# A fused attention and MLP kernel: local attention's loads issued by GpSimd, buffers turning over in program order, new priorities

## The chip, the cores and the metric

The kernel runs on one core of one Trainium2 chip. The metric is device time in microseconds (us) of one execution, and the median of several executions is what is compared. A profiled execution has a time of its own, beside the span that its trace covers.

## What is computed

The inputs q, k and v have 4 batches, 8 heads, 576 tokens and head size 64. Attention is a sum of two parts: softmax attention over tokens averaged in fours (144 pooled tokens), repeated four times, and softmax attention within a band of |i - j| < 4. Its output, as 2304 tokens of 512, goes through two MLPs with weights 512 x 2048 and 2048 x 512. Everything is float32.

```python
q_d = q.reshape(B, H, Sd, factor, D).mean(axis=3)          # k_d, v_d alike
out_up = np.repeat(sm_attn(q_d, k_d, v_d), factor, axis=2)
mask = np.abs(pos[:, None] - pos[None, :]) < factor
scores = np.where(mask, scale * np.matmul(q, k.transpose(0, 1, 3, 2)), -1000000000.0)
out_local = softmax(scores) @ v
x = (out_up + out_local).transpose(0, 2, 1, 3).reshape(2304, 512)
h = x @ w_in;  x = (h * np.cos(h)) @ w_out
h = x @ w_in2; r = np.maximum(h, 0.0);  out = (r * r) @ w_out2
```

## The kernel before

**The work and its tiles.** Every float32 product of the MLPs is made of three matmuls, high by high, high by low and low by high part (`mm3`, L665 to 668), so weights and activations are first split in a high and a low part. The first MLP runs over five rounds of 256 to 512 tokens, and in each over 16 blocks `f` of 128 hidden columns: `mlp_h` gives h, ScalarE and VectorE make h cos(h), `mlp_o` adds the block's share of the output. The weights come as 64-bit words, and `convert` makes one block of them: a load of `rawi` (w_in) or `rawo` (w_out) by SP (L291), three VectorE steps (L295, L302, L307), a copy on ScalarE and a subtraction on VectorE (`split`, L273 and L276). The second MLP runs over three blocks of 768 tokens with seven products for a pair of blocks (`big_h`, `big_o`).

**Attention** is cut in units that stand between the blocks of the MLP rounds, since a round needs only the tokens that it works on. A pooled unit (`unit_g`, one batch and a pair of heads) is S (L504), softmax, transposes T (L520), pv (L538) and a repeat (L544). A local unit (`unit_l`, one batch and 116 of its tokens; five in a batch, here l0 to l4) is a mask matmul (L573), S (L579), softmax, T (L592), a copy into `pz` (L596), pv (L616) and the addition that gives x (L642). Batch 0 has all pooled units and its first local ones ahead of the first MLP matmul.

**Loads of attention.** `load_pooled` brings the four strided quarters that are summed for the pooled q, k and v. For batch 0, SP loads q and k (L358, eight loads) and VectorE adds them up (L368, L375, L379); v comes by four GpSimd loads (L398), of which each adds to what the one before left in `vd_sb`, so they follow each other. For batches 1 to 3 all twelve are such GpSimd loads, behind a small GpSimd copy (`gate`, L391) that waits for a step of the work. `load_local` (L403 to 419) brings a local unit's q (L407), its k in two halves `kz` (L411) and its v (L414). There are two buffers of each: `kz_70` and `kz_71` by the unit's parity, `q` and `v` in turn. So the load for a unit waits until the unit two earlier has used its buffer.

**What sets the order.** The program is not written in the order in which it runs. `Plan.op` registers each step with engine, cost, a priority `key`, what it reads and writes and which new buffers it takes; to the key a number from the table `OFF` is added, by the step's name and the stage of the program. `Plan.order` (L104 to 203) then plays all steps through a model of the engines: on each engine the step that can start goes, of several the one with the lowest key. Buffers of some kinds (`IN_TURN`) must be taken in a fixed turn, which is the order of the keys. Where the model finds TensorE idle ahead of the first `mlp_o`, it puts in matmuls of zeros with 128 columns (`busy`, L1173, the tile `idle`), here called fills. The steps are issued in the order that comes out:

```python
for _, i in plan.order():
    if i < 0:
        busy()
    else:
        plan.ops[i][3]()
```

Of the kernel before, what the change touches and what calls it, by code (L numbers as in the profile page):

```python
# [16 lines left out]
B, H, S, D = 4, 8, 576, 64  # L17
NT, DM, DFF = 2304, 512, 2048
PR = H // 2
# [3 lines left out]
QT = 58  # L23
# [29 lines left out]
STG = (36, 140, 300, 440)  # L53


class Plan:


    RATE = {"SP": 1.24, "POOL": 2.07}
    LAT = {"PE": 0.15, "ACT": 0.15, "DVE": 0.15, "SP": 0.0, "POOL": 0.0}  # L60

    IN_TURN = ("rawi", "rawo", "w2", "p", "pt", "q", "v", "t", "w1")

    def __init__(self, bufs):
        self.bufs = bufs
# [42 lines left out]
    def order(self):  # L108
        ops, n = self.ops, len(self.ops)
        after = [[] for _ in range(n)]  # L110
        left = [0] * n
        for i, o in enumerate(ops):
            left[i] = len(o[4])
            for j in o[4]:
                after[j].append(i)
        ready_at = [0.0] * n
        end = [None] * n
        begin = [None] * n
        free = dict.fromkeys(self.LAT, 0.0)
        got = {t: [] for t in self.bufs}  # L120
        cand = {e: [i for i in range(n) if ops[i][0] == e and not left[i]] for e in free}
        table = [None]
        dma = adding = 0.0
        used, warm = {}, {0: False}
        self.fill = []
        out = []
        turn = {t: [] for t in self.bufs}
        for i in sorted(range(n), key=lambda i: (ops[i][2], i)):
            for inst in ops[i][5]:
                turn[inst[0]].append(inst)  # L130

        stream = [x for o in sorted(ops, key=lambda o: o[2]) for x in o[5] if x[1] == "ws"]

        def room(inst, more=0):
            tag = inst[0]
            held = got[tag]
            at = len(held) + more
            if tag in self.IN_TURN and turn[tag][at] != inst:
                return None
            if inst[1] == "ws" and stream[0] != inst:  # L140
                return None
            if at < self.bufs[tag]:
                return 0.0
            last = [end[i] for i in self.users[held[at - self.bufs[tag]]]]
            return None if None in last else max(last) + 0.1

        while len(out) < n:
            best = None
            for e, c in cand.items():
                t_min, pick = None, []  # L150
                for i in c:
                    t = max(free[e], ready_at[i])
                    for j, inst in enumerate(ops[i][5]):
                        x = room(inst, sum(o[0] == inst[0] for o in ops[i][5][:j]))
                        t = None if x is None or t is None else max(t, x)
                    if t is not None:
                        pick.append((t, i))
                if not pick:
                    continue
                t_min = min(pick)[0]  # L160
                pick = [
                    (ops[i][2] + (4.0 if ops[i][6] not in (None, table[0]) else 0.0), t, i)
                    for t, i in pick if t <= t_min + 0.02
                ]
                k, t, i = min(pick)
                if best is None or (t, k) < best[:2]:
                    best = (t, k, i)
            assert best is not None, "the plan is stuck"
            t, _, i = best
            e, cost, _, _, _, new, tb = ops[i]  # L170
            for inst in new:
                got[inst[0]].append(inst)
                if inst[1] == "ws":
                    stream.pop(0)
            begin[i] = t
            if tb is not None and tb != table[0]:
                t += 1.3
                table[0] = tb
            if e in ("SP", "POOL"):
                cost *= self.RATE[e]  # L180
                if e == "SP":
                    free[e] = t + 0.5
                    dma = max(dma, free[e]) + cost
                    end[i] = dma + 1.6
                else:
                    free[e] = t + 1.0
                    adding = max(adding, free[e]) + cost * (1.3 if dma > t else 1.0)
                    dma = max(dma, t) + cost
                    end[i] = adding + 2.0
            else:  # L190
                if e == "PE":
                    x = max(free[e], 0.8)
                    while self.idle and t - x > 0.35:
                        self.fill.append(x)
                        x += self.slow(used, warm, x, FILL)
                    if ops[i][3] is self.last_fill:
                        self.idle = False
                    cost = self.slow(used, warm, t, cost)
                free[e] = end[i] = t + cost
            cand[e].remove(i)  # L200
            out.append(i)
            for j in after[i]:
                left[j] -= 1
                lat = 0.07 if ops[j][0] == e else self.LAT.get(e, 0.0)
                ready_at[j] = max(ready_at[j], end[i] + lat)
                if not left[j]:
                    cand[ops[j][0]].append(j)
        self.end = max(end)
        return sorted([(begin[i], i) for i in out] + [(x, -1) for x in self.fill])
# [15 lines left out]
def body(ctx: ExitStack, tc: tile.TileContext, qb, kw, vw, qp, kp, vp, wi, wo, masks, ident, out_t):  # L225
    nc = tc.nc
# [18 lines left out]
    kz = [att.tile([128, 2, 2, PR, KT], F32, name=f"kz{i}") for i in range(2)]  # L245
# [17 lines left out]
    op = plan.op  # L263
    T = {}

    def new(inst, shape, dtype=F32, space=None):
        p = psum if space else att if inst[0] in ATT else pool
        T[inst] = p.tile(shape, dtype, tag=inst[0], name=inst[0], bufs=BUFS[inst[0]])
        return T[inst]
# [133 lines left out]
    def load_local(b, d, key):  # L403
        q, v, kt = ("q", b, d), ("v", b, d), (b * ND + d) % 2

        def lq():
            nc.sync.dma_start(out=new(q, [128, 2, PR, QT]), in_=qb[b, d])  # L407

        def lk(hh):
            pp = slice(64 * hh, 64 * hh + 64)  # L410
            nc.sync.dma_start(out=kz[kt][pp, hh], in_=kw[b, d, pp])  # L411

        def lv():
            nc.sync.dma_start(out=new(v, [128, 2, PR, D]), in_=vw[b, d])  # L414

        op("SP", 0.68, key, lq, w=[q], new=[q])
        for hh in range(2):
            op("SP", 0.4, key, lambda hh=hh: lk(hh), w=[("kz", kt, hh)])
        op("SP", 0.75, key + 0.5, lv, w=[v], new=[v])
# [778 lines left out]
    for n, r in enumerate(ORDER):  # L1198
# [9 lines left out]
        for f in range(NF):  # L1208
# [3 lines left out]
            if not last and f == (GATE if first else 0):  # L1212
                e = need(r + 1)
# [12 lines left out]
    for R in range(NBIG):  # L1226
        if R:
            operands(R, big_when[R - 1, 1], big_when[R - 1, 2], big_step * 5)
        for p in range(PAIRS):
# [3 lines left out]
            q = (R, p - 1) if p else (R - 1, PAIRS - 1)  # L1233
# [83 lines left out]
```

## Time and profile before

| | |
|---|---|
| median of 3 runs | 943.61 us (941.19, 943.61, 946.57) |
| profiled execution, its own time | 936.85 us |
| its span | 935.0 us |
| TensorE (PE) busy | 912.2 us, 98% of the span |
| VectorE (DVE) busy | 624.6 us, 67% |
| ScalarE (ACT) busy | 421.2 us, 45% |
| GpSimd (POOL) busy | 36.7 us, 4% |
| granted TensorE clock | 0.998 of full speed |

Busy times are sums over instructions of one engine, from the profiled execution. A share is an average over stages: the first 66 us, up to the first matmul of the MLP, hold the fills, and a matmul of zeros counts as busy like any other. Starts of instructions are in us from the start of the span. DMA-issuing instructions of SP (SPq) are short and count as no work; those of GpSimd stand among its instructions.

### The profile page before, as it was taken

The numbers are of one execution on the slowest core, as the hardware profiler recorded it, in microseconds if no ns is written. First come the engines' busy times: TensorE is split into PE (matmuls) and PEld (weight loads), VectorE is DVE, ScalarE is ACT, GpSimd is POOL, SyncE is SP. The second block draws the span as 40 slices with busy tenths as digits, with TensorE's granted clock in tenths as the row PEclk, the third lists the DMA queues.
The fourth block names the chain that finished last, engine by engine and source line by source line (L and its number), as shares of the span: only waits on it lengthen the run. The fifth ranks groups of instructions, "written<-read, shape, count | busy, mean of one in ns | idle before, by whom it ended". The sixth has DMA issues, their size and how long they took to land.

```text
span 935.0 us, 15239 instructions
## 1 busy us (share of the span) xinstructions
PE 912.2 (98%) x5794; PEld 793.7 (85%) x5794; DVE 624.6 (67%) x1106; ACT 421.2 (45%) x865; POOL 36.7 (4%) x53
## 2 busy tenths in 40 slices
PE   9999999999999999999999989999999999999997
PEld 9787787789788877888888879999999898999996
DVE  6898789744754269867897667878955454635351
ACT  1866568767766376656665522213221111121111
POOL 3001200220030000000000000000000000000000
PEclk9999999999999999999999999999999999999999
DMA  9876956994892255776897796878776555766543
GB/s 286 272 215 191 251 181 224 287 249 154 257 194 80 71 171 163 258 257 219 290 324 234 247 337 219 291 242 266 243 257 199 183 180 178 212 226 183 168 158 113
DMA packets 82569, 204.10 MB, mean 218 GB/s; under 512 B 9281, under 2 KB 18241, under 8 KB 82497
## 3 DMA queue, kind: packets, MB, share of 16 engines
q1 hardware_dynamic: 77888, 191.33, 62.1%
q0 software_dynamic: 4608, 11.80, 6.6%
q8 instruction: 46, 0.75, 0.3%
q14 instruction: 27, 0.21, 0.1%
HBM read 162.20 MB, written 40.89 MB: 217 GB/s over the span
## 4 chain that ended last, share of the span: by engine, by line
PE 72%; DMA 2%; ACT 1%; DVE 1%; issue 0%; SPq 0%; ACTq 0%; DVEq 0%
PE acc L666 9%; PE acc L667 9%; PE acc L668 9%; PE pp L666 6%; PE pp L667 6%; PE pp L668 6%; PE ps L666 5%; PE ps L667 5%; PE ps L668 5%; PE acx L1094 2%; PE acx L1095 2%; PE acx L1093 2%; DMA w<-w_dram 1%; PE ps L579 1%; PE ps L616 1%; PE ps L520 0%
## 5 line engine op out<-in xcount | busy, mean ns | idle before, releaser
L666 PE MATMUL ps<-xh,w 128*128 128x512 f32 (+1 forms) x320 | 120.8, 377 | 2.5 <-DVE t L706 1.9
L666 PE MATMUL acc<-gh,w 128*128 128x512 f32 (+1 forms) x320 | 120.3, 376 | 0.7 <-DMA w<-w_dram 0.7
L668 PE MATMUL acc<-gh,w 128*128 128x512 f32 (+1 forms) x320 | 118.1, 369 | 1.0 <-DVE w L276 1.0
L667 PE MATMUL ps<-xl,w 128*128 128x512 f32 (+1 forms) x320 | 118.0, 369 | 0.5 <-DVE xl L276 0.5
L668 PE MATMUL ps<-xh,w 128*128 128x512 f32 (+1 forms) x320 | 117.8, 368 | 0.0
L667 PE MATMUL acc<-gl,w 128*128 128x512 f32 (+1 forms) x320 | 117.8, 368 | 0.0
L276 DVE TENSOR_TENSOR gl<-t,gh 128x512 fp32r<-128x512 f32 (+1 forms) x80 | 50.7, 635 | 46.4 <-ACT gh L273 45.6
L706 DVE TENSOR_TENSOR t<-t,ps 128x512 f32<-128x512 f32 (+1 forms) x80 | 50.5, 632 | 39.3 <-ACT t L703 39.1
L1066 DVE TENSOR_TENSOR xl<-c,xh 128x768 fp32r<-128x768 f32 x32 | 30.6, 956 | 68.4 <-ACT xh L1063 68.2
L666 PEld LDWEIGHTS ps<-xh,w 128*128 128x128 f32 x320 | 60.2, 188 | 16.4 <-DVE t L706 3.6
L668 PEld LDWEIGHTS acc<-gh,w 128*128 128x128 f32 x320 | 60.3, 188 | 12.0 <-DVE w L276 1.8
L666 PEld LDWEIGHTS acc<-gh,w 128*128 128x128 f32 x320 | 60.3, 188 | 11.9 <-issue 1.4
L1025 DVE TENSOR_TENSOR c<-ua,pp 128x384 f32<-128x384 f32 x96 | 52.8, 552 | 24.9 <-PE pp L668 21.4
L667 PEld LDWEIGHTS ps<-xl,w 128*128 128x128 f32 x320 | 60.3, 188 | 10.2 <-DVE xl L276 0.9
L1063 ACT ACTIVATE xh<-c 128x768 fp32r<-128x768 f32 x32 | 27.0, 845 | 93.0 <-PE acc L668 84.6
L668 PEld LDWEIGHTS ps<-xh,w 128*128 128x128 f32 x320 | 60.3, 188 | 10.1
L667 PEld LDWEIGHTS acc<-gl,w 128*128 128x128 f32 x320 | 60.4, 189 | 9.4
L711 ACT ACTIVATE t<-t 128x512 f32<-128x512 f32 (+1 forms) x80 | 46.7, 585 | 47.9 <-DVE t L698 46.9
L694 ACT ACTIVATE ki<-ps 128x512 int32<-128x512 f32 (+1 forms) x80 | 43.6, 550 | 43.5 <-PE ps L668 35.8
L273 ACT ACTIVATE gh<-t 128x512 fp32r<-128x512 f32 (+1 forms) x80 | 46.6, 583 | 32.1 <-PE acc L668 27.5
L698 DVE SCALAR_TENSOR_TENSOR t<-ki,ps 128x512 f32<-128x512 int32 (+1 forms) x80 | 50.0, 629 | 7.7 <-ACT ki L694 6.9
L703 ACT ACTIVATE t<-t,halfpi 128x512 f32<-128x512 f32 (+1 forms) x80 | 54.1, 678 | 1.8
(163 smaller groups left out, 2103.2 us busy)
## 6 DMA issues: line engine op xcount, KB each, us to landing
w<-w_dram SPq DMA_DIRECT2D x96, 512.0 KB, 3.7
gl<-w_dram SPq DMA_DIRECT2D x84, 256.0 KB, 3.2
gh<-w_dram SPq DMA_DIRECT2D x84, 256.0 KB, 3.7
rawi<-in_wi_dram SPq DMA_DIRECT2D x32, 512.0 KB, 6.0
rawo<-in_wo_dram SPq DMA_DIRECT2D x32, 512.0 KB, 5.7
w_dram<-w SPq DMA_DIRECT2D x32, 512.0 KB, 4.9
w_dram<-rawo SPq DMA_DIRECT2D x24, 512.0 KB, 4.2
v<-in_vw_dram SPq DMA_DIRECT2D x20, 256.0 KB, 4.2
```

The costliest lines, as they stand in the source:

```text
L273: nc.scalar.activation(out=hi(), in_=src(), func=AF.Copy)
L276: nc.vector.tensor_tensor(out=lo(), in0=src(), in1=hi().bitcast(F32), op=OP.subtract)
L666: nc.tensor.matmul(ps, w_hi, r_hi, start=first, stop=False)
L667: nc.tensor.matmul(ps, w_hi, r_lo, start=False, stop=False)
L668: nc.tensor.matmul(ps, w_lo, r_hi, start=False, stop=last)
L694: nc.scalar.activation(out=tt(ki), in_=tt(hp), func=AF.Copy, scale=1.0 / TWO_PI)
L698: nc.vector.scalar_tensor_tensor(out=tt(t), in0=tt(ki), scalar=-TWO_PI, in1=tt(hp), op0=OP.mult, op1=OP.add)
L703: nc.scalar.activation(out=tt(t), in_=tt(t), func=AF.Sin, scale=-1.0, bias=halfpi[:, 0:1])
L706: nc.vector.tensor_tensor(out=tt(t), in0=tt(t), in1=tt(hp), op=OP.mult)
L711: "ACT", act(n), key + 0.2, lambda: nc.scalar.activation(out=tt(t), in_=tt(t), func=AF.Abs), w=[t]
L1025: nc.vector.tensor_tensor(out=out(), in0=a(), in1=ps(), op=OP.subtract if sub else OP.add)
L1066: nc.vector.tensor_tensor(out=gpart(1, R, f), in0=T[t], in1=gpart(0, R, f).bitcast(F32), op=OP.subtract)
```

## The change

The loads of local attention go from SP's queue to GpSimd's. In the planner they are an engine `GQ` of their own that shares GpSimd's time. Buffers of the kinds in `IN_TURN`, and those of the second MLP (`stream`), turn over in the order in which the program registers the steps, not in the order of the keys. The table `OFF` has new numbers throughout (211 entries before, 206 after; one is shown). All lines behind the planner stand 5 further down.

```diff
-OFF = {('SP|body.<lambda>|wid', 0): -8.1,
+OFF = {('SP|body.<lambda>|wid', 0): -56.0,
...
-    RATE = {"SP": 1.24, "POOL": 2.07}
-    LAT = {"PE": 0.15, "ACT": 0.15, "DVE": 0.15, "SP": 0.0, "POOL": 0.0}
+    RATE = {"SP": 1.24, "POOL": 2.07, "GQ": 1.24}
+    LAT = {"PE": 0.15, "ACT": 0.15, "DVE": 0.15, "SP": 0.0, "POOL": 0.0, "GQ": 0.0}
...
-        for i in sorted(range(n), key=lambda i: (ops[i][2], i)):
-            for inst in ops[i][5]:
+        for o in ops:
+            for inst in o[5]:
                 turn[inst[0]].append(inst)
-        stream = [x for o in sorted(ops, key=lambda o: o[2]) for x in o[5] if x[1] == "ws"]
+        stream = [x for o in ops for x in o[5] if x[1] == "ws"]
...
-            if e in ("SP", "POOL"):
+            if e in self.RATE:
                 cost *= self.RATE[e]
...
+                elif e == "GQ":
+                    free[e] = free["POOL"] = t + 1.0
+                    beside = max(beside, free[e]) + cost * (2.0 if dma > t else 1.0)
+                    dma = max(dma, t) + cost
+                    end[i] = beside + 1.8
                 else:
-                    free[e] = t + 1.0
+                    free[e] = free["GQ"] = t + 1.0
...
-            nc.sync.dma_start(out=new(q, [128, 2, PR, QT]), in_=qb[b, d])
+            nc.gpsimd.dma_start(out=new(q, [128, 2, PR, QT]), in_=qb[b, d])
...
-            nc.sync.dma_start(out=kz[kt][pp, hh], in_=kw[b, d, pp])
+            nc.gpsimd.dma_start(out=kz[kt][pp, hh], in_=kw[b, d, pp])
...
-            nc.sync.dma_start(out=new(v, [128, 2, PR, D]), in_=vw[b, d])
+            nc.gpsimd.dma_start(out=new(v, [128, 2, PR, D]), in_=vw[b, d])
...
-        op("SP", 0.68, key, lq, w=[q], new=[q])
+        op("GQ", 0.68, key, lq, w=[q], new=[q])
         for hh in range(2):
-            op("SP", 0.4, key, lambda hh=hh: lk(hh), w=[("kz", kt, hh)])
-        op("SP", 0.75, key + 0.5, lv, w=[v], new=[v])
+            op("GQ", 0.4, key, lambda hh=hh: lk(hh), w=[("kz", kt, hh)])
+        op("GQ", 0.75, key + 0.5, lv, w=[v], new=[v])
```

What comes out of the planner is shown at three places. The first is the start of SP's queue, before. `v`, `q` and `kz` are loads of local units, `rawi` and `rawo` weights, `up_sb` and `xr` the pooled q and k of batch 0.

```order
L414 DMA v<-in_vw_dram 128x512 x2
L291 DMA rawi<-in_wi_dram 128x1024 x2
L291 DMA rawo<-in_wo_dram 128x1024 x2
L1178 DMA mask_f<-in_masks_dram 128x192
L1176 DMA id_sb<-in_ident_dram 128x128
L407 DMA q<-in_qb_dram 128x464 x2
L358 DMA up_sb<-in_qp_dram 128x4x144 x4
L358 DMA xr<-in_kp_dram 128x4x144 x4
L411 DMA kz_70<-in_kw_dram 64x512
```

And after:

```order
L363 DMA up_sb<-in_qp_dram 128x4x144 x4
L363 DMA xr<-in_kp_dram 128x4x144 x4
L296 DMA rawi<-in_wi_dram 128x1024 x2
L1181 DMA id_sb<-in_ident_dram 128x128
L1183 DMA mask_f<-in_masks_dram 128x192
L296 DMA rawo<-in_wo_dram 128x1024 x2
L296 DMA rawi<-in_wi_dram 128x1024 x2
L296 DMA rawo<-in_wo_dram 128x1024
L342 DMA w_dram<-w_177 128x1024
```

The eight loads of pooled q and k went from behind ten others to the front, and local attention's loads are gone from this queue.

The second is the start of GpSimd's queue, before: `vd_sb` is the pooled v of batch 0, the memsets clear the buffers of the local units.

```order
L398 DMA vd_sb<-in_vp_dram 72x1024
L1185 MEMSET kz_70 64x512 x2
L1185 MEMSET kz_71 64x512 x2
L1188 MEMSET pz_72 128x928
L398 DMA vd_sb<-in_vp_dram 72x1024
L1188 MEMSET pz_73 128x928
L398 DMA vd_sb<-in_vp_dram 72x1024 x2
```

And after:

```order
L1190 MEMSET kz_70 64x512 x2
L1190 MEMSET kz_71 64x512 x2
L403 DMA vd_sb<-in_vp_dram 72x1024
L419 DMA v<-in_vw_dram 128x512 x2
L416 DMA kz_70<-in_kw_dram 64x512 x2
L416 DMA kz_71<-in_kw_dram 64x512
L403 DMA vd_sb<-in_vp_dram 72x1024
L416 DMA kz_71<-in_kw_dram 64x512
L1193 MEMSET pz_72 128x928
L1193 MEMSET pz_73 128x928
L412 DMA q<-in_qb_dram 128x464 x2
L403 DMA vd_sb<-in_vp_dram 72x1024
```

The four memsets of `kz` now stand ahead of the first pooled v, and loads of the local units l0 and l1 stand between the four loads of the pooled v; the third `q`, which waits for S of l0, comes next and stands ahead of the fourth.

The third is TensorE's queue in batch 2, from S of l2 to S of l4, before:

```order
L579 MATMUL ps<-kz_70,q 58x128 x8
L592 MATMUL ps<-id_sb,p 128x128 x8
L573 LDWEIGHTS id_68
L573 MATMUL ps<-mask_69,id_68 128x512
L579 MATMUL ps<-kz_71,q 58x128 x8
L616 MATMUL ps<-pz_72,v 64x116 x8
L616 MATMUL ps<-pz_73,v 64x116 x8
L573 LDWEIGHTS id_68
L573 MATMUL ps<-mask_69,id_68 128x512
L579 MATMUL ps<-kz_70,q 58x128 x8
```

And after (`kz_70` is the buffer of l2 and l4, `kz_71` that of l3):

```order
L584 MATMUL ps<-kz_70,q 58x128 x8
L597 MATMUL ps<-id_sb,p 128x128 x4
L621 MATMUL ps<-pz_72,v 64x116 x8
L578 LDWEIGHTS id_68
L578 MATMUL ps<-mask_69,id_68 128x512
L584 MATMUL ps<-kz_71,q 58x128 x8
L621 MATMUL ps<-pz_73,v 64x116 x8
L597 MATMUL ps<-id_sb,p 128x128 x4
L578 LDWEIGHTS id_68
L578 MATMUL ps<-mask_69,id_68 128x512
L584 MATMUL ps<-kz_70,q 58x128 x8
```

Both pv used to stand behind S of l3; now one stands ahead of it, and four of the eight transposes behind it.

In all there are 654 fills before and 508 after. Of those, 646 and 498 come ahead of the first matmul of the MLP, 350 and 72 ahead of the first S, and 249 and 210 between the first pooled pv and the first matmul of the MLP. Ahead of the split of x for the first MLP round, VectorE's queue has 12 conversions of weight blocks before and 9 after.

## Rows read from the trace of the kernel before

**Rows 1.** Windows: us, busy time (instructions) of each engine, clock, DMA share, GB/s.

```profile
0.00:20.00 20.00, 19.01 (x293) 19.01 (x294) 12.55 (x28) 3.81 (x5) 6.33 (x13) 1.00 0.93 283
66.00:935.00 869.00, 850.53 (x4888) 737.54 (x4885) 571.52 (x989) 383.41 (x723) 29.51 (x39) 1.00 0.68 215
```

**Rows 2.** Timeline of TensorE, first 67 us: start, us, instruction, count [idle before, releaser].

```profile
0.99 22.36 PE L1174 MATMUL idle<-zero 128*128 128x128 bf16 x350 [0.99 <-DVE zero L1168]
24.13 1.88 PE L504 MATMUL ps<-kd_sb,qd_sb 128*96 128x144 f32 x12 [0.78 <-DVE kd_sb L368]
...
27.52 2.40 PE L1174 MATMUL idle<-zero 128*128 128x128 bf16 x40
...
33.37 0.71 PE L538 MATMUL ps<-pt,vd_sb 72*64 72x144 f32 x8
...
66.07 0.48 PE L666 MATMUL ps<-xh,w 128*128 128x512 f32 x1
```

**Rows 3.** Timeline of VectorE, 10 to 25 us.

```profile
12.30 0.42 DVE L295 TENSOR_SCALAR wm<-rawo 128x512 int32<-128x512 int32 x1
...
14.57 0.25 DVE L1192 CAST mask<-mask_f 128x192 bf16<-128x192 f32 x1
...
17.14 0.64 DVE L375 TENSOR_TENSOR up_sb<-up_sb 128x144 f32<-128x144 f32 x2
```

**Rows 4.** Timeline of GpSimd, first 24 us.

```profile
1.28 0.70 POOL L398 DMA_DIRECT2D vd_sb<-in_vp_dram  x1 [0.84 <-POOLq L1307]
2.03 2.22 POOL L1185 MEMSET kz<- 64x512 f32 x4
...
6.58 0.83 POOL L398 DMA_DIRECT2D vd_sb<-in_vp_dram  x1 [1.53 <-DMA vd_sb<-in_vp_dram]
...
15.11 0.83 POOL L398 DMA_DIRECT2D vd_sb<-in_vp_dram  x1 [6.81 <-DMA vd_sb<-in_vp_dram]
21.89 0.83 POOL L398 DMA_DIRECT2D vd_sb<-in_vp_dram  x1 [5.95 <-DMA vd_sb<-in_vp_dram]
```

**Rows 5.** Timeline of GpSimd around 85 and 251 us, pooled loads of batches 1 and 3.

```profile
85.24 0.59 POOL L398 DMA_DIRECT2D qn_sb<-in_qp_dram  x1
...
88.65 0.91 POOL L398 DMA_DIRECT2D qn_sb<-in_qp_dram  x1 [1.74 <-DMA qn_sb<-in_qp_dram]
...
251.24 0.57 POOL L398 DMA_DIRECT2D kd_sb<-in_kp_dram  x1 [0.37 <-issue]
...
256.87 0.89 POOL L398 DMA_DIRECT2D kd_sb<-in_kp_dram  x1 [3.97 <-DMA kd_sb<-in_kp_dram]
...
259.85 0.84 POOL L398 DMA_DIRECT2D vd_sb<-in_vp_dram  x1 [0.18 <-issue]
```

**Rows 6.** Window of 66 to 106 us.

```profile
66.00:106.00 40.00, 38.09 (x174) 30.56 (x172) 36.53 (x64) 24.85 (x41) 8.47 (x12) 1.00 0.74 208
```

**Rows 7.** Timeline of TensorE in batch 2, 238 to 249 us.

```profile
238.60 1.09 PE L579 MATMUL ps<-kz,q 128*58 128x128 f32 x16
239.62 0.69 PE L520 MATMUL ps<-id_sb,p 96*72 96x96 f32 x6
...
241.38 0.66 PE L538 MATMUL ps<-pt,vd_sb 72*64 72x144 f32 x8
241.97 0.44 PE L520 MATMUL ps<-id_sb,p 96*72 96x96 f32 x3
...
245.03 1.09 PE L579 MATMUL ps<-kz,q 128*58 128x128 f32 x16
246.04 1.09 PE L592 MATMUL ps<-id_sb,p 128*128 128x128 f32 x8
...
247.28 1.09 PE L579 MATMUL ps<-kz,q 128*58 128x128 f32 x16
248.20 1.00 PE L616 MATMUL ps<-pz,v 128*64 128x116 f32 x16
```

**Rows 8.** Timeline of SP's queue there.

```profile
239.73 0.33 SPq L407 DMA_DIRECT2D q<-in_qb_dram  x1
```

More of the change, by code (lines that the diff above doesn't have):

```diff
@@ L122, in order @@
         table = [None]
-        dma = adding = 0.0
+        dma = adding = beside = 0.0
         used, warm = {}, {0: False}
```

2 lines of the change are left out of this document (1 added, 1 removed).

## The prediction, made before the changed kernel was run

> **What bounds the kernel now.** The windows of the trace come first [rows 1]: between 66 us, where the first layer of the first MLP begins, and the end, TensorE is busy for 850.53 of 869.00 us at a granted clock of 1.00. So 18.5 us of idle time is all that anything behind the start could give back as idle, and the other 850 us are matmuls whose number the change leaves as it is. The start is different. The timeline of TensorE [rows 2] shows that its busy first 23 us are fills: 350 of the 128-column matmuls that only keep it busy. The first real one, S of pooled attention, begins at 24.13 and was released by VectorE's add of the pooled keys; the first pooled pv comes at 33.37 and the first matmul of the MLP at 66.07. What the change moves in the first 66 us, and what it does to the loads of local attention later, decides the time.
>
> The sum is made against the profiled execution, 936.85 us (span 935.0). The median of the three runs, 943.61, is 0.7% above it and the three lie between 941.19 and 946.57, so I work out a difference and carry it to the median. About 0.5%, 4.7 us, is what a measurement of this kernel can tell from no change.
>
> **1. The start.** Before, SP sends v, two w_in and two w_out blocks, mask, identity and q of two units, and only then the eight loads of pooled q and k; after, those eight are its first. Each is 128x4x144 numbers of 4 bytes, 0.29 MB, so q is 1.18 MB, which takes 4.2 us at the 283 GB/s of the first 20 us [rows 1]. VectorE's adds of q began at 17.14 and S was freed at 24.13 [rows 2, 3], 7.0 us later, other steps among them. From 1 us on this gives the first S at about 12 instead of 24.13. Its program agrees: 72 fills ahead of that S instead of 350.
>
> This is not yet a gain, for what is late next is the fourth load of the pooled v, without which no pooled pv runs. These four are a chain on GpSimd, each adding to the one before: issued at 1.28, 6.58, 15.11 and 21.89 [rows 4], 20.6 us from the first to the last. In the change the four memsets of 2.22 us come ahead of the first, which therefore goes out at about 3.5, and the fourth at 24.1. A mean step of the chain is 6.9 us, so it lands at about 31.0. The five issues of v and kz put between the first two cost 2.9 us at 0.57 (issues of loads that add nothing took 0.57 to 0.59 [rows 5]) and fit inside the first step of 5.3. From the first pooled pv to the MLP it took 32.7 us (33.37 to 66.07) [rows 2]; the program now has 39 fills fewer in that stretch, at 0.060 each (40 in 2.40 [rows 2]) 2.3 us, and one T of 0.5 us has moved ahead of it. 31.0 + 32.7 - 2.3 - 0.5 = 60.9 against 66.07: **-5.2 us**. Fills that stand in that wait cost nothing while they are shorter than it. Ends: all 148 fills that are left out ahead of the MLP were on the path, 148 x 0.060 = -8.9; or the 1.5 MB of local loads that GpSimd now sends between the first and third of the chain hold it up by their 5.4 us at 283 GB/s, +0.2.
>
> **2. Three weight conversions come later.** Ahead of the split of x for the first MLP, VectorE converts 12 weight blocks before and 9 after. One is four operations, from 12.30 to 14.57, 2.27 us [rows 3]; three are 6.8 us in the stretch of 66 to 106, where VectorE is busy for 36.53 of 40 us [rows 6], so 3.5 are free there. Ends: 0 (they wait until later, where VectorE has room: 571.52 of 869 us [rows 1]) and 6.8 - 3.5 = +3.3. Not all are due in that stretch; I take a third, **+1.0**.
>
> **3. Local attention's loads on GpSimd.** There are two q and two kz buffers, so the load for a unit waits for the S two units earlier. Before, for batch 2, S of unit 0 ends at 239.62, SP issues at 239.73, and S of unit 2 starts at 245.03 [rows 7, 8]: a turn of 5.4 us, just covered by what TensorE has between them. The change lets GpSimd issue the same three loads (q and two halves of kz). No row shows that; the nearest are its plain pooled loads, three in a row. At 251.24 the next link of the first went out after 5.6 us and that of the third after 8.6; at 85.24 the first took 3.4 [rows 5]. These three move 0.88 MB, a unit's three 0.50 MB, so I take 5.6, between ends of 3.4 and 8.6. Now the work between such pairs, in batch 2's order after, at the pitches of TensorE there [rows 7]: between unit 0 and 2 there are as many steps as before less one group of three plus seven transposes, 5.4 us; between 1 and 3 the eight pooled pv groups (2 x 0.59), T, mask and S (1.76), four and four transposes with a mask (1.24), a local pv (1.00), 5.2 us; between 2 and 4 the same 1.24, S 0.92, two local pv 2.0 and a mask 0.4, 4.6 us. A stall also lengthens the next interval: 0.2 for unit 2, 0.2 for unit 3, 5.6 - 4.6 - 0.2 = 0.8 for unit 4. Sum **+1.2**. In batches 1 and 3 the order leaves two or three more MLP groups in between, 6.3 us and more, and covers 5.6. Ends: at 3.4 nothing; at 8.6 3.2 + 0.2 + 3.8 in batch 2, 2.3 in batch 3 and about 1 in batch 1, +10.5.
>
> The Trainium skill bears on this in "SBUF — State Buffer", section "SBUF: two separate sides": GpSimd writes its own DMA descriptors and is kept from it while VectorE runs a two-port copy, so loads should go out on SP or ScalarE. Here GpSimd's plain issue took 0.59 us at 85.24 [rows 5] in a stretch with VectorE 91% busy [rows 6], which does not bear the rule out; it is priced as a rival.
>
> **4. The rest.** SP loses 80 issues, some 0.33 us each [rows 8], but TensorE has only those 18.5 us of idle time behind the start [rows 1], and no row shows any of it to hang on these issues; nothing is put down as gained. The turning over of buffers in program order changes neither the order of the second MLP's matmuls nor that of the tail: 0.
>
> Sum: -5.2 + 1.0 + 1.2 = -3.0. From the median this is 943.61 - 3.0 = **940.6 us**; the profiled execution would become 933.9.
>
> **Rivals.**
> **A. All of the start arrives.** The chain of pooled v runs faster because SP's 3.3 MB of other early loads no longer go ahead of it, conversions and turns hide: -8.9, 934.7 us. For it: the steps of 8.5 and 6.8 behind the first of 5.3 [rows 4] fall where SP's queue is full. Against it: the local loads now share GpSimd's queue. With some of the 18.5 us of idle time going too, down to 932.
> **B. The turns stall TensorE.** A GpSimd turn takes 8.6 us as its third load at 251 did [rows 5]: +10.5 and +1.0, less 5.2, is +6.3, 949.9 us. It is slower by over 4.7 from a turn of about 8.2 us on. Against it: 0.88 MB in those rows against 0.50. Without the gain at the start, 955.
> **C. The start stays at 66.** Queue order behind the pooled v, as bounded above: +0.2 + 1.0 + 1.2, 946 us.
> **D. VectorE slows the issues.** Adding loads show issues of 0.91 us against 0.59 [rows 5], 0.3 more; three in a turn make it 6.6: batch 2 loses 1.2 + 0.2 + 1.8, batch 3 0.3, together +3.5: 943.6 - 5.2 + 1.0 + 3.5 = 942.9 us. That is the rule of the Trainium skill's page; its own figures, about 620 ns alone and 3100 overlapped ("A bandwidth-pool intuition that's wrong"), would by an estimate from that page put 7.5 us on a turn and the time beyond B's.
>
> **How the numbers follow.** Forecast 0.36, A 0.34, B 0.16, C 0.09, D 0.05. The forecast's own spread (a few us both ways, between the ends of part 1) puts a small share of it, 0.03, below -4.7 and 0.02 above +4.7. Faster by over 0.5%: 0.34 + 0.03 = 0.37. Slower: 0.16 + 0.02 = 0.18. Within 0.5%: what is left of the forecast, 0.31, with C and D, 0.45. The range takes in A with its lower end and B: 932 to 951; left out are B without the gain at the start and what is faster than all fills, some 0.15.
>
> **What would show it.** In the changed profile: the first pooled S near 12, the first pooled pv near 31, its releaser the fourth pooled v; the first MLP matmul near 61. In the waits, TensorE waits for kz or q 1 to 2 us in all, in batch 2; plain GpSimd issues of about 0.6. VectorE's share in the 40 us behind the first MLP matmul goes up. Wrong would be: a first MLP matmul under 58 (A) or over 65 (C), waits for kz and q of over 8 us (B), or issues over 0.8 us (D), or a change behind 300 us, where I put nothing.

## The result and the profile after

The changed kernel takes 952.89 us (median of 6 runs, 948.96 to 956.31) against 943.74 us for the kernel before (6 runs, 939.12 to 946.57). The ratio is 1.0101, with a 95% interval of 1.0065 to 1.0136: it is slower by 1.0%, beyond the 940.6 us of the forecast and beyond its range. The profiled execution took 952.43 us (span 950.6), near its median, while that of the kernel before, 936.85, was a low one. So the two traces differ by 15.6 us where the medians differ by 9.2, and a stretch of one trace is compared below with several traces of the same order.

The first part of the page, after:

```profile
PE 911.5 (96%) x5648; PEld 791.2 (83%) x5648; DVE 623.7 (66%) x1106; ACT 423.9 (45%) x869; POOL 80.8 (8%) x133
```

TensorE's busy time hardly moved from 912.2 us, though 146 fills are gone: what is left runs longer, at a lower granted clock (0.988 of full speed in the mean, 0.998 before). Its idle time is 39.1 us against 22.8. The windows (columns as in [rows 1]) say where, for the start and for two stretches around 200 us:

```profile
0.00:70.00 70.00, 59.37 (x781) 53.47 (x782) 50.78 (x114) 37.19 (x142) 22.52 (x42) 0.95 0.82 236
180.00:200.00 20.00, 19.15 (x143) 18.83 (x144) 9.76 (x29) 11.19 (x27) 9.13 (x12) 0.91 0.83 171
200.00:210.00 10.00, 6.15 (x35) 5.98 (x35) 1.90 (x5) 2.88 (x8) 1.07 (x2) 0.70 1.00 255
```

In 0 to 70 us TensorE is idle for 10.6 us and its clock is 0.95; before, it was idle for 4.3 us at 1.00. From 200 to 210 us it is busy for 6.15 us only, at a clock of 0.70. TensorE's timeline in the first 66 us answers to [rows 2]:

```profile
0.99 6.54 PE L1179 MATMUL idle<-zero 128*128 128x128 bf16 x72 [0.99 <-DVE zero L1173]
15.17 3.19 PE L509 MATMUL ps<-kd_sb,qd_sb 128*96 128x144 f32 x12 [7.65 <-DVE kd_sb L373]
...
28.06 1.09 PE L584 MATMUL ps<-kz,q 128*58 128x128 f32 x16
29.08 5.92 PE L1179 MATMUL idle<-zero 128*128 128x128 bf16 x103
35.47 0.63 PE L597 MATMUL ps<-id_sb,p 128*128 128x128 f32 x4 [0.46 <-DVE p L478]
36.06 1.20 PE L543 MATMUL ps<-pt,vd_sb 72*64 72x144 f32 x16
...
65.83 0.47 PE L671 MATMUL ps<-xh,w 128*128 128x512 f32 x1
```

72 fills instead of 350, and then nothing for 7.65 us: the first S waits for the sums of the pooled k and starts at 15.17. Its twelve matmuls take 3.19 us where they took 1.88, since the clock had gone down in the wait (granted clock 0.50 from 13 to 19 us). The first pooled pv comes at 36.06, right behind T of l0 and without a wait of its own, later than the 33.37 of before, and the first matmul of the MLP at 65.83 against 66.07. GpSimd's timeline answers to [rows 4]:

```profile
2.90 0.69 POOL L403 DMA_DIRECT2D vd_sb<-in_vp_dram  x1
...
19.06 0.89 POOL L403 DMA_DIRECT2D vd_sb<-in_vp_dram  x1 [4.69 <-DMA vd_sb<-in_vp_dram]
29.45 0.56 POOL L412 DMA_DIRECT2D q<-in_qb_dram  x1 [9.50 <-PE ps L584]
30.00 0.90 POOL L403 DMA_DIRECT2D vd_sb<-in_vp_dram  x1
```

The third load of the pooled v goes out at 19.06, the fourth only at 30.00: the third `q` in front of it waited 9.50 us for S of l0. The list of TensorE's waits (us in total, times, longest):

```profile
PE ps L509 <- DVE kd_sb L373: 7.6, 1, 7.6
PE acc L671 <- DMA w<-w_dram: 3.8, 1, 3.8
PE acx L1098 <- DMA w<-w_dram: 3.7, 6, 1.1
PE ps L671 <- DVE t L711: 3.5, 4, 1.8
PE ps L671 <- ACT xh L278: 1.8, 1, 1.8
```

No wait for `q` or `kz` is in the list. The costly new one behind the start is a single wait of 3.8 us for a weight block.

To see where the time went, I read from each trace when the first matmul of the MLP starts, and when that of its third round (round 2, the first with 512 columns again behind the 256 of round 1) starts. The table has the results of all kernels tried below too; "old" and "new" tell whose order the steps stand in.

| kernel | order, local loads by | first MLP matmul | from it to round 2 | round 2 to the end | ratio to before |
|---|---|---|---|---|---|
| before | old, SP | 66.07 | 186.9 | 682.1 | 1 |
| e2_gq | old, GpSimd | 68.37 | 186.3 | 681.2 | 1.0005 |
| e6_turn | old, other turn, SP | 68.91 | 190.3 | 681.9 | 0.9992 |
| e12_before_no_adds | old, SP | 69.98 | 188.6 | 682.9 | 0.9995 |
| after | new, GpSimd | 65.83 | 199.7 | 685.1 | 1.0101 |
| e1_sp | new, SP | 65.22 | 199.2 | 686.9 | 1.0081 |
| e5_warm | new, GpSimd | 65.59 | 201.3 | 685.4 | 1.0098 |
| e10_late_local | new, GpSimd | 70.24 | 198.4 | 683.3 | 1.0117 |
| e11_no_adds | new, GpSimd | 64.75 | 192.7 | 684.2 | 1.0037 |
| e30_sp_early | new, SP | 66.24 | 192.8 | 684.4 | 1.0060 |
| e31_gq_early | new, GpSimd | 68.86 | 198.4 | 683.1 | 1.0101 |
| e20_stage2 | mixed, GpSimd | 67.78 | 197.6 | 685.1 | 1.0051 |
| e21_stage4 | mixed, GpSimd | 64.40 | 195.9 | 686.5 | 1.0102 |
| e22_start_only | mixed, GpSimd | 64.42 | 199.3 | 703.7 | 1.0290 |

The loss stands in rounds 0 and 1: from the first MLP matmul to round 2 it takes 198 to 201 us in after, e1_sp, e5_warm and e10_late_local, instead of 186 to 190 in the old order. Most of it is round 1, 86 us in after instead of 75. The end adds about 3 us. The start gives some 2 us back: in the seven traces that have the new start unchanged (all new and mixed ones but e5_warm, e10_late_local and e22_start_only) the first MLP matmul comes at 64.4 to 68.9, 66.2 in the mean, in the four of the old order at 66.1 to 70.0, 68.3 in the mean. Before's own is the earliest of these four.

### The profile page after: what moved, and what is told of

It is laid out like the page before. It is cut to its first block, busy times and chain, and to the rows that moved or that the text cites. A ratio compares the mean times of both kernels' runs of the same rounds, so it can differ in the third digit from the quotient of the medians.

```text
span 950.6 us, 15033 instructions
## 1 busy us (share of the span) xinstructions
PE 911.5 (96%) x5648; PEld 791.2 (83%) x5648; DVE 623.7 (66%) x1106; ACT 423.9 (45%) x869; POOL 80.8 (8%) x133
## 4 chain that ended last, share of the span: by engine, by line
PE 77%; DMA 8%; DVE 8%; ACT 6%; issue 1%; SPq 0%; DVEq 0%; ACTq 0%
PE acc L671 10%; PE acc L673 10%; PE acc L672 10%; PE ps L671 6%; PE ps L672 6%; PE ps L673 6%; PE pp L671 6%; PE pp L673 5%; PE pp L672 5%; DMA w<-w_dram 4%; PE acx L1098 2%; PE acx L1099 2%; PE acx L1100 2%; ACT p L456 1%; PE ps L621 1%; PE idle L1179 1%
## 5 line engine op out<-in xcount | busy, mean ns | idle before, releaser
L671 PE MATMUL acc<-gh,w 128*128 128x512 f32 (+1 forms) x320 | 122.3, 382 | 5.9 <-DMA w<-w_dram 3.8
L673 PE MATMUL acc<-gh,w 128*128 128x512 f32 (+1 forms) x320 | 119.5, 373 | 0.8 <-DVE w L281 0.8
L671 PEld LDWEIGHTS ps<-xh,w 128*128 128x128 f32 x320 | 61.6, 193 | 18.5 <-DVE t L711 5.5
L673 PEld LDWEIGHTS ps<-xh,w 128*128 128x128 f32 x320 | 61.6, 192 | 10.1
L1030 DVE TENSOR_TENSOR ua<-ua,pp 128x384 f32<-128x384 f32 x72 | 39.8, 552 | 32.8 <-PE pp L673 29.7
```

Source lines behind the costliest of these rows:

```text
L671: nc.tensor.matmul(ps, w_hi, r_hi, start=first, stop=False)
L673: nc.tensor.matmul(ps, w_lo, r_hi, start=False, stop=last)
L1030: nc.vector.tensor_tensor(out=out(), in0=a(), in1=ps(), op=OP.subtract if sub else OP.add)
```

## The experiments

**Queue or order.** Two kernels split the change: the new order with SP's loads, and the old order with GpSimd's.

```diff
-            nc.gpsimd.dma_start(out=new(q, [128, 2, PR, QT]), in_=qb[b, d])
+            nc.sync.dma_start(out=new(q, [128, 2, PR, QT]), in_=qb[b, d])
...
```

(`kz` and `v` alike; in the second kernel the other way round, in the kernel before.)

> The changed kernel with its own order, but local attention's loads issued by SP again, at the places that they have in the program's order. TensorE's, VectorE's and ScalarE's queues are those of the changed kernel. Theory order (the new order of the steps costs the time, above all in the second round of the first MLP): stays within 0.4% of the changed kernel, ratio to before 1.007 to 1.014, TensorE again waits 2 us or more for a weight block near 205 us, and the first MLP matmul of the third round comes near 265 us. Theory queue (GpSimd's slower issue or landing costs it): ratio to before at most 1.003 and the third round near 255 us.

> The kernel before with its own order, but local attention's loads issued by GpSimd. Theory order: within 0.3% of before (0.997 to 1.003), no wait of TensorE for q or kz above 1 us in all. Theory queue: 1.006 or more, with waits of TensorE for q, kz or v, or for the pooled v whose chain stands on the same queue.

Measured: 1.0081 (1.0049 to 1.0112) for the new order with SP's loads, 1.0005 (0.9987 to 1.0022) for the old order with GpSimd's. The queue costs nothing that can be told, in either order; the loss comes with the order. In the trace of the first, the wait for a weight block was 1.94 us, just under the 2 us expected, and round 2 starts at 264.4; in that of the second, TensorE waits for `kz` for 1.0 us in all, the bound that I had given. The tile `q` in the trace after and in that before tells why the queue is harmless: GpSimd's issue takes 0.57 us (median), and from issue to landing it is as fast as SP.

```profile
L412 POOL DMA_DIRECT2D q<-in_qb_dram x20: 536/565/928, 12.9 to 365.4; - x20
...
DMA to landing us min/median/max: 2.8/4.2/9.2
```

```profile
L407 SPq DMA_DIRECT2D q<-in_qb_dram x20: 327/338/756, 5.5 to 352.1; - x20
...
DMA to landing us min/median/max: 2.6/4.4/9.7
```

**The turning over alone**, in the kernel before:

```diff
-        for i in sorted(range(n), key=lambda i: (ops[i][2], i)):
-            for inst in ops[i][5]:
+        for o in ops:
+            for inst in o[5]:
...
-        stream = [x for o in sorted(ops, key=lambda o: o[2]) for x in o[5] if x[1] == "ws"]
+        stream = [x for o in ops for x in o[5] if x[1] == "ws"]
```

> The kernel before with buffers turning over in program order, its table of priorities and SP's loads as before. Theory order, the table alone: the rule of turning over matters little under the old table, ratio 0.997 to 1.004. Rival: the rule itself makes steps wait for their buffer's turn, ratio 1.005 or more, with longer waits of TensorE for weights.

Measured 0.9992 (0.9974 to 1.0011). So what makes the order is left: the new table of priorities, together with the planner's engine `GQ`. No kernel here takes these two apart.

**The adding loads beside the weights.** In the trace after, the weight block that TensorE waits for from 201.65 to 205.50 us is asked for at 196.49 and lands 8.88 us later. SP's queue, the DMA view of 185 to 210 us (queues: packets, MB, share of the 16 engines; then issues, KB each, median us to landing), and TensorE's timeline there:

```profile
196.49 13.54 SPq L350 DMA_DIRECT2D w<-w_dram  x4
```

```profile
q0 software_dynamic: 1307, 3.17, 72.9%
q1 hardware_dynamic: 430, 1.57, 18.1%
...
w<-w_dram SPq DMA_DIRECT2D x4, 512.0 KB, 9.4
kd_sb<-in_kp_dram POOLq DMA_DIRECT2D x3, 288.0 KB, 5.8
vd_sb<-in_vp_dram POOLq DMA_DIRECT2D x3, 288.0 KB, 6.7
qn_sb<-in_qp_dram POOLq DMA_DIRECT2D x3, 288.0 KB, 7.5
```

```profile
201.37 0.28 PE L673 MATMUL ps<-xh,w 128*128 128x256 f32 x1
205.50 0.55 PE L671 MATMUL acc<-gh,w 128*128 128x256 f32 x1 [3.85 <-DMA w<-w_dram]
205.84 0.41 PE L672 MATMUL acc<-gl,w 128*128 128x256 f32 x1
206.06 0.41 PE L673 MATMUL acc<-gh,w 128*128 128x256 f32 x1
...
210.75 0.28 PE L671 MATMUL ps<-xh,w 128*128 128x256 f32 x1
210.87 0.28 PE L672 MATMUL ps<-xl,w 128*128 128x256 f32 x1
```

Pooled q, k and v of batch 2, nine of whose twelve loads add to what is there, hold 72.9% of the DMA engines' time, and a weight block takes 9.4 us. Behind the wait of 3.85 us the 256-column matmuls come 0.21 us apart instead of 0.12 for 5 us, at the lower of the clock's two levels (1.2 instead of 2.4 GHz). I left the nine adding loads out, in the changed kernel and, as a control, in the kernel before:

```diff
-                    "POOL", 0.82, key, lambda dst=dst, src=src, r=r, how=how: nc.gpsimd.dma_start(
+                    "POOL", 0.82, key, lambda dst=dst, src=src, r=r, how=how: None if b == 2 and r else nc.gpsimd.dma_start(
```

> The changed kernel without the nine adding loads of batch 2's pooled q, k and v (their sums are left out, only the first quarter is loaded). Theory contention (these loads, which run from 186 to 206 us, slow the weight block that TensorE waits 3.8 us for at 205 us, and the clock is at half for about 5 us behind that wait): the wait falls under 1 us, the granted clock of 200 to 210 us rises from 0.70 to 1.00, and the time falls by 4 to 7 us, ratio to before 1.003 to 1.006. Rival (the block is asked for too late in the new order, whatever else is loaded): the wait stays above 2.5 us and the time within 2 us of the changed kernel.

> The kernel before without the same nine adding loads of batch 2's pooled q, k and v (their sums are left out). Theory contention through order (the old order has the same loads, but keeps the weight blocks clear of them): the time falls by less than 2.5 us, ratio to before 0.997 to 1.001, and round 1 to round 2 stays at 74 to 76 us. Rival (the adding loads cost 6 us wherever they stand, and the new order has nothing to do with it): 4 us or more are gained, ratio 0.996 or below, round 1 to round 2 in 71 us or less.

Measured: 1.0037 (1.0014 to 1.0060) in the new order, 944.61 us, and 0.9995 (0.9981 to 1.0010) in the old one. The same nine loads cost 6 us in the one (some 2 to 10, going by the two intervals) and under 2 in the other. The window and the weight loads of the changed kernel without them:

```profile
200.00:210.00 10.00, 9.37 (x75) 8.90 (x74) 4.24 (x11) 4.77 (x12) 0.00 (x0) 1.00 0.43 154
```

```profile
w<-w_dram SPq DMA_DIRECT2D x6, 512.0 KB, 3.3
```

The clock is back at 1.00, the wait is gone and a block lands in 3.3 us.

Why the loads cost nothing in the old order is not what I had expected there, that it keeps the weight blocks clear of them. In the trace before, three weight blocks are asked for from 194.67 on, while the adding loads still run. GpSimd's last of them and SP's queue, then how long these three blocks took to land and, below it, the same for the three from 196.49 on in the trace after:

```profile
198.06 0.84 POOL L398 DMA_DIRECT2D vd_sb<-in_vp_dram  x1 [1.03 <-DMA vd_sb<-in_vp_dram]
```

```profile
194.67 3.19 SPq L345 DMA_DIRECT2D w<-w_dram  x3
```

```profile
DMA to landing us min/median/max: 6.9/8.4/11.3
```

```profile
DMA to landing us min/median/max: 8.9/9.8/10.2
```

And TensorE's timeline before, where the first and the last of the three are first used:

```profile
204.09 0.28 PE L666 MATMUL acc<-gh,w 128*128 128x256 f32 x1
...
208.93 0.39 PE L666 MATMUL acc<-gh,w 128*128 128x256 f32 x1 [0.32 <-DMA w<-w_dram]
```

So the blocks land late in both orders. What differs is how long TensorE has other work: in the old order the first block is used 9.4 us after it was asked for, two local pv and four transposes being among what stands in between, and only the third is waited for, 0.32 us. In the new order the block is wanted 5.2 us after it was asked for (201.65 less 196.49), and takes 8.9. That this lead decides is read from the traces; no kernel here changes it alone.

**Moving them earlier.** If it is their place, 10 us earlier should help. In the new order their gate waits for a softmax of batch 1's third local unit and opens at 181.67 (174.17 before); the last pooled pv that reads their buffers is done at 172.

```diff
-        for _, i in plan.order():
+        line = [i for _, i in plan.order()]
+        adds = [i for i in line if i >= 0 and i in early]
+        last = max(line.index(i) for i in range(adds[0]) if ("pv", i) in reads)
+        for i in adds:
+            line.remove(i)
+        line[last + 1:last + 1] = adds
+        for i in line:
```

(`early` holds batch 2's pooled loads, `reads` batch 1's pooled pv; batch 2's gate copy is dropped.)

> The kernel of the first experiment (changed order, local attention's loads on SP), with batch 2's twelve pooled loads taken off their gate and put right behind the last pooled pv of batch 1, the last step that reads their buffers: they can run from 172 us instead of 182. Theory contention (what the new order costs is mostly these loads beside the weight loads of round 1): they end by 194 to 198 us, before or with the first weight loads at 196, TensorE's wait there goes from 2 to 4 us to under 1, round 1 to round 2 takes 78 to 81 us instead of 85, and the time falls by 3 to 6 us, ratio to before 1.002 to 1.005. Rival (they only move their contention onto loads ahead of them): ratio 1.007 or more, other waits for DMA in place of that one.

> The same with the changed kernel itself, its local loads on GpSimd: the loads of the last units of batch 1 now stand behind the adding loads on GpSimd's queue. Theory contention: as with SP's loads, ratio 1.002 to 1.006, since the q, kz and v behind them are wanted only 20 us later. Rival (one queue in order: TensorE waits for q, kz or v of these units): more than 1 us of such waits and a ratio above 1.008.

Measured: 1.0060 (1.0037 to 1.0083) with SP's local loads, against 1.0081 without the move, and 1.0101 (1.0077 to 1.0125) with GpSimd's. The first did in its trace what was expected (the block lands in 6.1 us, the wait is 1.06 us, from the MLP's start to round 2 it takes 6 us less), but its median fell by 2.4 us only, less than the 3 to 6 expected, and the intervals overlap; its trace, 945.17 us, is below its median of 947.48, and that of e1_sp, 953.12, above its own of 949.89. So that the place of these loads costs time is not shown by it, though the trace points that way. The second did not: TensorE waits as before, and not for the local loads but for the weights.

```profile
207.88 0.55 PE L676 MATMUL acc<-gh,w 128*128 128x256 f32 x1 [4.19 <-DMA w<-w_dram]
```

```profile
kz<-in_kw_dram POOLq DMA_DIRECT2D x4, 128.0 KB, 13.4
...
q<-in_qb_dram POOLq DMA_DIRECT2D x2, 232.0 KB, 12.6
```

On GpSimd's queue in order, seven local loads stood behind the adding ones, went out together from 197.05 on, and came into the DMA engines beside the same weight blocks: `kz` took 13.4 us to land. Here the queue did matter, in the trace; in the times the two intervals, 1.0037 to 1.0083 and 1.0077 to 1.0125, just overlap.

**The start.** Two kernels on the new order: the eight early local loads put behind the third load of the pooled v, and 110 more fills behind the first 72.

```diff
-        for _, i in plan.order():
+        line = [i for _, i in plan.order()]
+        own = [i for i in line if i >= 0 and plan.ops[i][0] in ("POOL", "GQ")]
+        adds = [i for i in own if plan.ops[i][0] == "POOL" and plan.ops[i][1] > 0][:4]
+        held = [i for i in own if plan.ops[i][0] == "GQ" and own.index(i) < own.index(adds[2])]
+        for i in held:
+            line.remove(i)
+        at = line.index(adds[2]) + 1
+        line[at:at] = held
```

```diff
+                seen += 1
+                if seen == 72:
+                    for _ in range(110):
+                        busy()
```

> The changed kernel, but the eight loads of local attention that GpSimd issues ahead of its third load of the pooled v go behind that one. Theory start (these loads take the DMA engines from the pooled k that SP asked for first): the first pooled S comes at 10 to 12 us instead of 15.2, and TensorE's 7.6 us wait there shrinks to 3 or 4; but the first MLP matmul moves by less than 2 us, because then S of the first local unit waits for q or kz, as it does with SP's loads. Rival (the pooled k is late for SP's own queue): the first S stays at 14 us or later. Rival two (the late pooled k alone holds the start): the first MLP matmul at 62 us or earlier. Time within 0.4% of the changed kernel unless rival two holds, then 3 to 4 us less.

> The changed kernel with 110 more fills behind the first 72, in the 7.6 us in which TensorE waits for the pooled k. Theory: the first S still starts at 14 to 16 us, since it waits for VectorE's sums, but at the full clock, so that its twelve matmuls take 1.9 us instead of 3.2 and the first MLP matmul comes 1 to 2 us earlier, at 63.5 to 65; granted clock of the first 70 us 0.98 or more instead of 0.95; ratio to before 1.006 to 1.011. Rival (these fills are on the path): the first MLP matmul 3 us or more later. Rival two (the fills the plan left out were worth nothing, warm or cold): the same time within 0.5 us at the first MLP matmul.

With the local loads held back the first S came at 10.08, as expected: they had taken the DMA engines from the pooled k. But S of l0 then waited 8.40 us for its `q`, more than expected, and the MLP started at 70.24 instead of within 2 us of 65.83; ratio 1.0117 (1.0087 to 1.0147).

```profile
10.08 0.98 PE L509 MATMUL ps<-kd_sb,qd_sb 128*96 128x144 f32 x6 [3.32 <-DVE kd_sb L373]
...
31.42 1.97 PE L584 MATMUL ps<-kz,q 128*58 128x128 f32 x16 [8.40 <-DMA q<-in_qb_dram]
...
40.43 1.20 PE L543 MATMUL ps<-pt,vd_sb 72*64 72x144 f32 x16
```

With SP's loads (e1_sp) it was the same in small: S at 10.58, a wait of 4.31 us for `q`, the MLP at 65.22. With more fills the clock stayed at 1.00 and six matmuls of S took 0.93 us (the first S came at 13.13, ahead of the 14 to 16 expected), but the MLP came at 65.59, 0.2 us earlier: rival two of that run. Its pv waited for the pooled v:

```profile
13.13 0.93 PE L509 MATMUL ps<-kd_sb,qd_sb 128*96 128x144 f32 x6
...
36.13 1.20 PE L543 MATMUL ps<-pt,vd_sb 72*64 72x144 f32 x16 [0.28 <-DMA vd_sb<-in_vp_dram]
```

So in the trace after three chains end within 1 us of each other: the fills behind S of l0 at 35.00, the softmax of l0 at 35.32, which T of l0 waits for, and the fourth pooled v, which lands at 35.93. Taking one away shows the next. In e1_sp, where no `q` stands ahead of it, the fourth pooled v goes out at 26.40 and lands 4.6 us later, at 31.0, and the pooled pv still starts at 35.39, behind the fills and T of l0:

```profile
26.40 0.82 POOL L403 DMA_DIRECT2D vd_sb<-in_vp_dram  x1 [7.73 <-DMA vd_sb<-in_vp_dram]
```

```profile
28.37 6.64 PE L1179 MATMUL idle<-zero 128*128 128x128 bf16 x103
34.85 0.61 PE L597 MATMUL ps<-id_sb,p 128*128 128x128 f32 x4
35.39 1.20 PE L543 MATMUL ps<-pt,vd_sb 72*64 72x144 f32 x16
```
The ratio with more fills is 1.0098 (1.0064 to 1.0133), the same as the changed kernel.

**Which numbers of the table.** Three kernels take the numbers of some stages from the old table: those of rounds 1 and 2, those of the second MLP, and all but those of the start. One entry of the first:

```diff
-('GQ|load_local.lq|q|wq', 2): 9.4,
+('GQ|load_local.lq|q|wq', 2): 126.7,
...
```

> The changed kernel, but the table's 39 numbers for the steps of rounds 1 and 2 of the first MLP (its second and third) are those of before; GpSimd's loads, the turning over and the rest of the table stay. If the second round's order is what costs (theory order, with the adding loads of batch 2 beside the weight loads as its largest part), the stretch from the first matmul of round 1 to that of round 2 falls from 86 us to 75 to 79, and the time by 6 to 11 us, ratio to before 0.998 to 1.004. Rival (the loss comes from rounds 0 and the start, and would turn up anywhere): the stretch stays above 83 us and the ratio above 1.007.

> The changed kernel, but the table's numbers for the second MLP are those of before. From the last first-layer matmul of the first MLP to the end it took 410 to 412 us in kernels with the new order and 407 with the old: if these numbers do it, 407 to 408 and ratio to before 1.004 to 1.008; if it is something earlier that shifts the loads there, 410 or more and 1.008 to 1.013.

> The changed kernel, but all of the table except the numbers for the start (what comes ahead of the first MLP matmul) is that of before; GpSimd's loads and the turning over stay. Theory order: 0.996 to 1.003, the first MLP matmul at 64 to 67 us, since the new start gains nothing there, and round 1 to round 2 in 75 to 79 us. Rival (the new start is worth its 5 us and only what follows gave it back): the first MLP matmul by 62 us and ratio 0.996 or below.

Old numbers for rounds 1 and 2 gave 1.0051 (1.0031 to 1.0070), half of the loss; the stretch from round 1 to round 2 took 81.7 us, above the 75 to 79 expected (its trace, 952.32 us, is the longest of its twelve executions). Old numbers for the second MLP gave 1.0102 (1.0059 to 1.0145): no gain, and 411 us for the last part, so my reading of the 3 us there fell. All old but the start gave 1.0290 (1.0256 to 1.0323), which neither theory had: the first MLP matmul at 64.42 as expected, but then new waits that neither kernel has.

```profile
130.66 0.80 PE L671 MATMUL ps<-xh,w 128*128 128x512 f32 x1 [5.06 <-DVE t L711]
```

```profile
469.68 1.09 PE L597 MATMUL ps<-id_sb,p 128*128 128x128 f32 x4 [4.72 <-DVE p L478]
```

In this last kernel the old numbers behind a new start make waits of their own, so mixing is no way to tell stages apart, and the half that e20_stage2 gives is not more than a hint.

## Why the prediction was wrong

**Part 4 failed: "the rest", 0 us.** I priced the three edits of the diff and what they moved at the start and in the local units, and put nothing on the new order in rounds 0 and 1 of the first MLP. My first paragraph asked only how much of the 18.5 us of idle time could be given back, and took the 850 us of matmuls behind the start as fixed; both can also grow. That is where 13 us of the traces' 15.6 went (9 to 13 against the traces of the old order). Without batch 2's adding loads the new order loses 0.4% instead of 1.0%, and the old order loses nothing by them. So about two thirds of the loss, by the middle values, comes of these loads in the new order. They meet round 1's weight blocks in both orders, and the blocks land 7 to 11 us after they are asked for; but in the new order TensorE wants the first of them after 5.2 us instead of 9.4. That a wait there also lowers the clock added to it: 3.85 us of idle, and then some 5 us of matmuls at almost half the pace (granted clock 0.50). The rows for it were in the trace of before: the three blocks from 194.67 on, which landed up to 11.3 us after they were asked for, covered by other work. I used the chains of adding loads [rows 4, 5] to price a turn of local loads, and did not ask what else would be loading when they ran, and how soon TensorE would want it.

**Part 1 failed too: -5.2, measured -0.2** in these two traces, and some -2 in the mean of the traces of either order. From the first pooled pv to the MLP I worked out 29.9 us and it took 29.8. Two steps failed. One is "the fourth at 24.1": I shifted the old spacing of the chain by the memsets, and left out that a `q` which waits for S of l0 stands right ahead of that load in the same queue, so that it went out at 30.00. The other is the path itself, that the pooled pv starts when this load lands. In e1_sp it lands at 31.0, the very time that I had worked out, and the pv starts at 35.39: T of l0 had moved ahead of that pv, as I had noted, and I priced its 0.5 us but not the softmax that it waits for, nor the fills. The first S at 12 came at 15.17, because the local loads took the DMA engines from the pooled k (10.08 without them). And the sentence that fills cost nothing in a wait was right, but I did not see its other side: where 278 fills went, TensorE stood still for 7.65 us and lost its clock.

**Part 2, +1.0:** from the MLP's start to round 1 it took 113.6 us instead of 111.8, but 115.1 in e6_turn, whose conversions are the old ones. The sign that I gave is there (VectorE is busy for 38.99 of the 40 us from 66 on, instead of 36.53), but what it costs can't be told.

**Part 3, +1.2, measured 0.** GpSimd's loads of q, kz and v land in 3.9 to 4.4 us (medians) and no turn was waited for. 5.6 was too much because I took it from three pooled loads that start together. Rival B, the only case that I gave as clearly slower, had the sign and the wrong cause: its sign to look for, waits for q and kz of over 8 us, is not there. Rival D fell too: the 80 issues of these loads took 0.52 to 0.93 us, 0.53 to 0.57 in the median, and not over 0.8 as a rule. The rule of the Trainium skill in "SBUF — State Buffer", section "SBUF: two separate sides", that GpSimd is kept from writing its descriptors while VectorE runs a two-port copy, is neither borne out nor refuted by that, since no run shows which of VectorE's steps here are such copies. Rival A's start, under 58, did not come. Rival C, with the start over 65, had its time right; but in e1_sp the chain of the pooled v is not held up by local loads, and the MLP starts at 65.22 all the same, so its reason was not needed.

**What stays open.** The new order without the adding loads is still 0.4% behind. Some of that is waits which the order makes in every trace of it with no numbers mixed (1.8 us for `xh` ahead of round 1, 1.8 us for `t` within it, 1.4 to 1.6 us for a weight's high part in round 0), and some 2 to 4 us lie in the second MLP, where TensorE is idle for 1.8 to 5.3 us of 600 to 900 us, against 0 to 0.8 in the four traces of the old order. What puts them there I did not find. Nor is it shown whether the table or the planner's engine `GQ` gives TensorE less other work ahead of the blocks. None of the kernels beats the one before.

## What to carry to other kernels

A new table of priorities is an edit of every stage: go through each queue from end to end for what now runs at the same time, and price two transfers that meet by their landing times when they do, not by the time of each alone, and hold that against the work that the engine has until it wants them. When a queue in order takes over more work, look at what stands behind each entry that waits for another engine, here the last pooled v behind a `q`. Filling matmuls that are taken out are a gain only where something else is ready to run in their place.

## What the hardware showed that I had not expected

- Adding loads cost the DMA engines twice as much for each byte: from 185 to 210 us GpSimd's queue, most of it such loads, took 72.9% of 25 us for 3.17 MB, SP's weights 18.1% for 1.57 MB, so 5.7 against 2.9 us of all engines for a MB. It is not GpSimd's queue as such: in e11_no_adds its plain loads took 47.9% of the 8 us from 181 on for 1.22 MB, 3.1 us for a MB. A weight block beside adding loads landed in 9.4 us, without them in 3.3 (medians).
- Behind waits of TensorE of 1.4 to 8.6 us in the new order the clock was often granted at its lower level for some us (0.70 in 200 to 210 us), so that a wait cost more than its length; without the adding loads, and so without the wait of 3.85 us, that stretch stood at 1.00. It does not follow every wait: behind the same 1.82 us ahead of round 1 the clock went down in the trace after and not in that of e11_no_adds. The old order has such stretches too, fewer of them (three in e6_turn, none in the trace before until its last 4 us).
- How long the wait near 205 us is differs from trace to trace: 3.85, 1.94, 3.26 and 4.19 us in after, e1_sp, e5_warm and e31_gq_early. Each is one execution of another kernel, so what of that comes from the edit and what from the execution can't be told.
